# First weight tile on a second queue, an early filling matmul removed, and four output transfers halved, in a scan and gated-FFN kernel

## The chip, the cores and the metric

One core of one Trainium2 chip. The metric is the device time of one execution, in microseconds (us), from the first to the last instruction of the program. Engines are TensorE (PE), VectorE (DVE), ScalarE (ACT), GpSimd (POOL) and SyncE (SP); SP and ACT also issue transfers, which run on the core's 16 DMA engines.

## The reference

The input x is 2048 tokens of 512 values in bfloat16. It is normalised over the 512 values; from the result two branches are computed and joined:

```python
xn = _layernorm(x, axis=-1)
# s: state-space scan, 512 complex states over 2048 tokens
dt = exp(log_dt); Lam_bar = exp(dt * Lam); B_bar = ((Lam_bar - 1) / Lam)[:, None] * Bmat
Bu = einsum("bld,pd->blp", xn, B_bar)
h[t] = Lam_bar * h[t-1] + Bu[:, t]                       # for t in range(2048)
s = 2 * einsum("blp,dp->bld", h, Cmat).real + xn * Dskip
# g: gated feed-forward, inner width 1376
g = silu((gelu(xn @ w_gate) * (xn @ w_up)) @ w_down)
out = x + s * g
```

## The kernel before, in words

The 2048 tokens are cut into 4 slabs of 512 and each slab into 4 tiles of 128 (M = 4, written m; slabs are s). All weights stay in on-chip memory. A slab goes through these stages: the tiles are normalised and turned (`xna` to `xnT`, by a transposing transfer for whole slabs); gate and up products per tile (`gate_tile`, L433), multiplied on VectorE into `at`; `at` is turned to `atT` by a transposing transfer (`at_t`, L449); the down product from `atT` (L465); the state inputs (L528), rotated by tables, scanned along the tokens on VectorE (L559) and rotated back into `hst`; and the read-out (L481), multiplied by the gate and added to x (`y_part`, L486 and L491), from which a transfer writes 128 rows of the output (L494).

Nothing is scheduled while the kernel runs. Each step is recorded with what it reads and writes (`Plan.add`), and `Plan.run` emits the steps in the order of a list written out by hand, `ORDER`; the cost figures given with the steps play no part in it. So every engine has a fixed order, and an engine waits, in that order, on semaphores. Eight semaphores are shared by all transfers in the order of issue: a transfer takes the semaphore of the one eight issues before, and is issued after that one has landed.

The first slab has no time for a transposing transfer, so its head is done another way, and this is where most of the change lies:

- SP's queue starts with the loads of x tiles 0, 1 and 2, then the row tiles of `w_up` (`wu`, 128 rows of the first 1024 columns, 256 KB each; row tile k is what `up_rows(m, k)` multiplies), x tile 3, and the rest. ACT's queue starts with three small loads of the scan's parameters (`pv0`, `pv1`).
- `dummies(7, 3)` gives TensorE seven matmuls on constants from the start (L295), before any data is there.
- `center(0)` sums tile 0 in two parts, on DVE (columns 0 to c, L340) and ACT (the rest, L338), and DVE subtracts the mean (L342). `center(m)` for the other tiles sums on ACT (L346) and subtracts on DVE (L347).
- `head_t(0)` turns tile 0 by four transposes on TensorE (L312), copied out by DVE (L318) and ACT (L320) into `xcT`, a view of `W`. `parameters` turns the parameter rows (L584, L585), copied out by DVE (L587, `pf`). `fill(1, 0)` adds one matmul on constants (L301). `head_t(1)` to `head_t(3)` turn the other tiles (L327, copied by L329).
- `up_rows(m, k)` multiplies tile m by row tile k of `w_up`, two matmuls of 512 columns (L382); the sums leave by ACT (`out_up`, L391), scaled by 1/deviation, which comes later from GpSimd (`rstd`).
- After that `first_gates` does the gate products of slab 0, and its four tiles go through `at_t`.

At the end, the last tile's read-out is done in two halves of 256 columns, each with its own output transfer; `ot` has two buffers, used by even and odd tiles.

Of the kernel before, what the change touches and what calls it, by code (L numbers as in the profile page):

```python
# [10 lines left out]
AF = mybir.ActivationFunctionType  # L11
# [7 lines left out]


ORDER = (
    19, 24, 17, 18, 16, 14, 15, 13, 25, 0, 20, 12, 21, 1, 22, 2, 23, 3, 4, 27, 26, 5, 39, 6, 28, 7, 29, 41, 30, 33, 40, 60, 8, 34, 31, 61, 35, 32, 42,
    9, 63, 46, 62, 65, 133, 64, 45, 66, 131, 69, 68, 36, 37, 50, 57, 134, 51, 67, 52, 48, 10, 54, 70, 53, 49, 71, 56, 72, 73, 79, 43, 58, 76, 80, 44,
    82, 137, 77, 74, 38, 95, 147, 75, 81, 91, 78, 85, 97, 92, 55, 84, 47, 198, 135, 86, 93, 87, 59, 149, 88, 199, 151, 103, 138, 94, 83, 107, 96, 98,
    153, 216, 136, 155, 99, 101, 220, 104, 139, 11, 217, 140, 100, 109, 111, 102, 119, 106, 108, 214, 221, 105, 115, 110, 156, 132, 117, 120, 154, 90,
    218, 125, 112, 150, 116, 113, 215, 123, 114, 219, 222, 122, 141, 126, 127, 160, 164, 118, 148, 124, 89, 121, 179, 128, 143, 275, 161, 162, 165,
    158, 223, 224, 166, 163, 181, 227, 167, 129, 157, 130, 142, 152, 229, 226, 144, 183, 185, 225, 233, 168, 180, 228, 283, 280, 279, 182, 237, 159,
    169, 358, 186, 170, 184, 172, 200, 235, 171, 234, 173, 201, 241, 174, 238, 276, 243, 282, 175, 176, 258, 244, 259, 236, 277, 239, 245, 177, 278,
    178, 281, 187, 240, 246, 296, 264, 242, 202, 247, 292, 260, 284, 285, 265, 204, 188, 297, 203, 302, 262, 189, 293, 261, 191, 311, 286, 190, 248,
    303, 298, 205, 263, 192, 317, 307, 312, 300, 308, 230, 206, 299, 294, 301, 207, 295, 232, 208, 231, 305, 304, 318, 306, 352, 322, 315, 326, 209,  # L30
    210, 316, 327, 313, 320, 211, 193, 418, 309, 310, 330, 332, 212, 314, 341, 195, 331, 323, 290, 324, 328, 325, 287, 196, 337, 213, 329, 339, 288,
    197, 345, 319, 289, 353, 194, 333, 291, 146, 335, 334, 347, 354, 359, 336, 364, 338, 145, 365, 343, 360, 321, 249, 250, 355, 346, 340, 356, 342,
    376, 426, 377, 380, 366, 254, 378, 393, 381, 344, 394, 349, 382, 397, 348, 420, 350, 361, 253, 362, 351, 379, 383, 252, 398, 369, 395, 410, 421,
    251, 425, 419, 396, 256, 424, 411, 414, 435, 257, 416, 415, 357, 370, 266, 436, 443, 450, 444, 423, 417, 267, 412, 422, 375, 255, 427, 428, 269,
    445, 413, 399, 451, 429, 446, 441, 439, 460, 458, 271, 400, 440, 454, 461, 442, 270, 437, 455, 268, 448, 432, 438, 456, 481, 475, 273, 430, 465,
    452, 459, 274, 272, 471, 479, 453, 367, 371, 433, 457, 363, 480, 447, 463, 482, 462, 431, 372, 368, 434, 476, 502, 373, 484, 473, 466, 500, 503,
    384, 472, 486, 374, 492, 496, 449, 385, 493, 388, 386, 387, 501, 537, 477, 497, 474, 478, 523, 467, 483, 389, 494, 519, 498, 487, 495, 468, 524,
    499, 390, 469, 485, 525, 488, 551, 526, 489, 504, 391, 505, 520, 507, 539, 521, 552, 464, 508, 392, 522, 490, 506, 401, 513, 514, 402, 535, 403,
    553, 538, 536, 405, 406, 557, 515, 509, 555, 558, 404, 541, 569, 563, 556, 540, 408, 407, 542, 409, 554, 564, 559, 527, 565, 619, 561, 528, 562,
    560, 570, 624, 531, 530, 567, 578, 574, 575, 625, 568, 566, 576, 518, 620, 584, 577, 532, 585, 572, 510, 529, 511, 580, 591, 516, 533, 599, 582,  # L40
    583, 579, 589, 581, 571, 491, 573, 517, 587, 621, 597, 622, 586, 593, 595, 598, 600, 626, 623, 588, 629, 534, 634, 614, 615, 594, 630, 612, 543,
    596, 592, 590, 613, 544, 617, 610, 608, 604, 601, 545, 606, 635, 607, 627, 609, 605, 512, 602, 631, 603, 611, 641, 470, 616, 547, 628, 618, 639,
    548, 647, 642, 546, 643, 549, 645, 550, 636, 637, 632, 648, 646, 638, 633, 652, 640, 653, 649, 650, 657, 651, 644, 658, 654, 662, 667, 655, 656,
    663, 659, 668, 660, 664, 661, 665, 669, 666, 670, 671,
)


# [33 lines left out]
def kernel(  # L81
# [79 lines left out]
    tF = sb("tF", [P, 2, D], FP32)  # L161
    junks = [sb(f"junk{i}", [P, D]) for i in range(2)]
    junk_n = [0]

    def junk():
        junk_n[0] += 1
# [11 lines left out]
    def dve(n, emit, reads=(), writes=(), rate=1.0, base=DV, **kw):  # L178
        return pl.add(DVE, base + n / 960.0 / rate, emit, reads, writes, lag=0.13, **kw)

    def acts(n, emit, reads=(), writes=(), ptr=0, **kw):
        return pl.add(ACT, AC + 0.12 * ptr + n / 1200.0, emit, reads, writes, lag=0.16, **kw)

    def pe(n, cols, emit, reads=(), writes=(), **kw):
        return pl.add(PE, n * (cols + 6) / 2400.0, emit, reads, writes, lag=0.22, **kw)
# [4 lines left out]
    def dma(eng, issue, land, emit, reads=(), writes=(), **kw):  # L190
        return pl.add(eng, issue, emit, reads, writes, lag=land, **kw)
# [17 lines left out]
    def load_w(nm, k0, k1, c0, c1, end, landed):  # L209

        w, r = w_of[nm]
        dma_sp(end, landed, lambda: nc.sync.dma_start(out=w[:, k0:k1, c0:c1], in_=r[:, k0:k1, c0:c1]),
               [(nm, k, c) for k in range(k0, k1) for c in range(3) if c0 <= CH[c][0] < c1])
# [10 lines left out]
    load_x(0, 1.12, 2.92)  # L224
    load_x(1, 1.59, 3.35)
    load_x(2, 2.06, 3.75)
    load_w("wu", 0, 1, 0, W2, 2.53, 5.1)
    load_w("wu", 1, 2, 0, W2, 3.0, 6.3)
    load_w("wu", 2, 3, 0, W2, 3.5, 7.4)
    load_x(3, 4.0, 7.75)  # L230
# [18 lines left out]
        early.append(dve(32, lambda i=i: V.memset(at[i][:, F:FP], 0.0), writes=[("atpad", i)], rank=900.0))  # L249
    one = nc.const_aps.tensor(1.0, [P, 1], FP32)  # L250

    first = [acts(1, lambda: act(out=tiny[:], in_=one, func=AF.Silu), [], ["tiny"], rank=910.0, not_before=0.72)]
    for i, (t, v) in enumerate(((pv0[0:4, :], A_log_dt), (pv1[0:4, :], A_Lambda_im), (pv1[4:8, :], A_Lambda_re))):
        first = [dma(ACT, 0.48, 1.7, lambda t=t, v=v: A.dma_start(out=t, in_=v.rearrange("(k p) -> k p", p=P)),
                     writes=[("pv", i)], rank=900.0, not_before=0.8, after=first)]
    iota_i = sb("iota_i", [P, NBA], I32)
    iota_f = small("iota_f", NBA)

# [36 lines left out]
                T.matmul(ybank[j][:] if j < 2 else ring[i][:], lhsT=warm[:, 0:P], rhs=warm, start=True, stop=True)  # L295
        pl.add(PE, k * 0.427, f, [], [("bank", i), ("y", 0), ("y", 1)], lag=0.22, not_before=0.6)

    def fill(k, i):
        def f():
            for _ in range(k):  # L300
                T.matmul(ring[i][:], lhsT=warm[:, 0:P], rhs=warm, start=True, stop=True)  # L301
        pe(k, 512, f, [], [("bank", i)])

    def head_t(m):

        if m == 0:
# [26 lines left out]
    def center(m):  # L333

        x = x_tok[:, m, :]
        if m == 0:
            c = 3 * P
            acts(D - c, lambda: act(out=junk()[:, 0 : D - c], in_=x[:, c:D], func=AF.Copy, scale=1.0 / D, accum_out=mb[:, 0:1]),  # L338
                 [("x", 0, 0)], ["mb"], ptr=1, rank=400.0)
            dve(c, lambda: V.tensor_scalar(out=yg[0][:, 0:c], in0=x[:, 0:c], scalar1=1.0 / D, scalar2=None, op0=ALU.mult, op1=ALU.add,  # L340
                                           accum_out=ma[:, 0:1]), [("x", 0, 0)], [("yg", 0, 0), ("ma", 0)], base=0.15, rank=400.0, after=early)
            head.append(dve(512, lambda: V.tensor_scalar(out=xn[0], in0=x, scalar1=ma[:, 0:1], scalar2=mb[:, 0:1], op0=ALU.subtract, op1=ALU.subtract),  # L342
                            [("x", 0, 0), ("ma", 0), "mb"], [("xc", 0, 0), ("xc", 0, 1)], rate=2.3, rank=400.0, after=head[-1:]))
            return
        nmean, key = ma[:, m : m + 1], ("ma", m)
        sums0.append(acts(512, lambda: act(out=junk()[:], in_=x, func=AF.Copy, scale=-1.0 / D, accum_out=nmean), [("x", 0, m)], [key], ptr=2, rank=400.0 - 20 * m))  # L346
        dve(512, lambda: V.tensor_scalar(out=xn[m], in0=x, scalar1=nmean, scalar2=None, op0=ALU.add),  # L347
            [("x", 0, m), key], [("xc", m, 0), ("xc", m, 1)], rate=2.3, rank=330.0 - 20 * m)
# [123 lines left out]
    def y_part(s, m, c0, c1, bank, key, seed, e):  # L472
# [14 lines left out]
        else:  # L487
            ys = tF[:, 0, c0:c1]
            dve(w, lambda: V.tensor_tensor(out=ys, in0=ps, in1=sk[s % 2][:, m, c0:c1], op=ALU.add), [key, ("sk", s % 2, m)], [("tF",)])
            dve(w, lambda: V.tensor_tensor(out=yg[e][:, c0:c1], in0=ys, in1=g2[gi][:, b, c0:c1], op=ALU.mult), [("tF",), ("g2", gi, b)], [("yg", e, c0)])  # L490
        dve(w, lambda: V.tensor_tensor(out=ot[e][:, c0:c1], in0=yg[e][:, c0:c1], in1=x_tok[:, s * M + m, c0:c1], op=ALU.add),  # L491
            [("yg", e, c0), ("x", s, m)], [("ot", e, c0)], rate=2.0)
        mg = s * TS + m * P
        dma(SP, 0.35, 1.5, lambda: nc.sync.dma_start(out=out_td[mg : mg + P, c0:c1], in_=ot[e][:, c0:c1]), [("ot", e, c0)], [("out", s, m, c0)], svc=(2, 0.4, 0.9))  # L494

    def y_tile(s, m):
        i = y_n[0] % 2
# [143 lines left out]
    rstd(0, 1)  # L641
    for m in range(1, M):
        norms = rstd(m, m + 1)
    fill(1, 0)
    head_t(1)
    up_rows(0, 0)
    up_rows(1, 0)
# [174 lines left out]
```

## Time and profile before

| | us |
|---|---|
| median of 3 runs | 179.16 |
| lowest and highest run | 178.5, 179.44 |
| the profiled execution: its span from the first to the last instruction | 178.6 |
| time shown around that span | none |
| PE busy in it | 173.4 |
| DVE busy | 156.4 |
| ACT busy | 125.2 |
| POOL busy | 12.0 |

The profile comes from one more execution, beside the three timed ones; its span is given with one digit and has no other time beside it. Busy time of PE is that of matmuls, whose ends are modelled; instructions that issue transfers are not counted as busy. In the chain of waits each line is a stretch of the work that ended last: when it starts, how long it is, and the engine with the tile that it writes. In a timeline each line is a group of instructions with its start, its length, and in brackets the idle time of the engine before it and what ended that.

### The profile page before, as it was taken

The numbers are of one execution on the slowest core, as the hardware profiler recorded it, in microseconds if no ns is written. First come the engines' busy times: TensorE is split into PE (matmuls) and PEld (weight loads), VectorE is DVE, ScalarE is ACT, GpSimd is POOL, SyncE is SP. The second block draws the span as 40 slices with busy tenths as digits, with TensorE's granted clock in tenths as the row PEclk, the third lists the DMA queues.
The fourth block names the chain that finished last, engine by engine and source line by source line (L and its number), as shares of the span: only waits on it lengthen the run. The fifth ranks groups of instructions, "written<-read, shape, count | busy, mean of one in ns | idle before, by whom it ended". The sixth has DMA issues, their size and how long they took to land.

```text
span 178.6 us, 2428 instructions
## 1 busy us (share of the span) xinstructions
PE 173.4 (97%) x850; PEld 82.8 (46%) x850; DVE 156.4 (88%) x252; ACT 125.2 (70%) x240; POOL 12.0 (7%) x25
## 2 busy tenths in 40 slices
PE   7999999899999999999999999999999999999992
PEld 2555544344445544444445454444444455444451
DVE  3729999999599995899979999899999999999663
ACT  6679999797998999889578865373148618582340
POOL 2462040000200000000040000000000000000000
PEclk9999999999999999999999999999999999999999
DMA  5999999999000809814000075094000006536111
GB/s 159 338 372 188 176 227 315 150 211 228 2 0 0 196 2 173 110 59 81 0 0 6 6 124 129 25 195 84 0 0 0 0 29 155 69 58 135 53 64 60
DMA packets 47507, 18.66 MB, mean 104 GB/s; under 512 B 40232, under 2 KB 46472, under 8 KB 47496
## 3 DMA queue, kind: packets, MB, share of 16 engines
q1 hardware_dynamic: 47472, 18.52, 48.6%
q8 instruction: 6, 0.10, 0.3%
q14 instruction: 5, 0.04, 0.1%
q10 hardware_dynamic: 24, 0.00, 0.0%
HBM read 6.46 MB, written 2.10 MB: 48 GB/s over the span
## 4 chain that ended last, share of the span: by engine, by line
PE 81%; DVE 7%; DMA 6%; ACT 2%; POOL 0%; issue 0%; DVEq 0%
PE ring L433 31%; PE ring L465 20%; PE ybank L481 15%; PE ring L528 12%; DMA atT<-at 5%; PE ring L382 3%; ACT at L391 2%; DVE st L278 1%; DVE Q L620 1%; DMA x_tok<-in_A_x_dram 1%; DVE at L415 1%; DVE yg L486 1%; DVE tab L620 1%; DVE ot L491 1%; DVE sk L364 1%; ACT junk L351 0%
## 5 line engine op out<-in xcount | busy, mean ns | idle before, releaser
L433 PEld LDWEIGHTS <-xnT 128*128 128x128 bf16 x288 | 28.2, 98 | 28.4
L465 PE MATMUL ring<-wd,atT 128*128 128x512 bf16 (+1 forms) x176 | 39.5, 379 | 0.8 <-DMA atT<-at 0.7
L433 PE MATMUL ring<-wg,xnT 128*128 128x512 bf16 (+1 forms) x144 | 31.6, 357 | 0.0
L433 PE MATMUL ring<-wu,xnT 128*128 128x512 bf16 (+1 forms) x144 | 31.3, 357 | 0.0
L528 PE MATMUL ring<-xnT,BT 128*128 128x512 bf16 x128 | 30.1, 379 | 0.0
L559 DVE TENSOR_TENSOR_SCAN Fs<-rho,ini,W 128x512 bf16<-128x512 f32 x24 | 29.7, 1270 | 0.1
L436 ACT ACTIVATE ub<-ring 128x512 bf16<-128x512 f32 (+1 forms) x36 | 19.2, 555 | 14.1 <-PE ring L433 14.0
L481 PE MATMUL ybank<-C,hst 128*128 128x512 bf16 x120 | 27.7, 379 | 0.0
L465 PEld LDWEIGHTS <-atT 128*128 128x128 bf16 (+1 forms) x176 | 17.1, 98 | 22.1 <-DMA atT<-at 1.2
L530 ACT ACTIVATE U<-ring 128x512 bf16<-128x512 f32 x32 | 18.3, 601 | 8.0 <-PE ring L528 8.0
L436 ACT ACTIVATE gt<-ring 128x512 bf16<-128x512 f32 (+1 forms) x36 | 19.5, 555 | 3.7 <-PE ring L433 3.5
L481 PEld LDWEIGHTS <-hst 128*128 128x128 bf16 x136 | 13.3, 98 | 14.0
L528 PEld LDWEIGHTS <-BT 128*128 128x128 bf16 x128 | 12.5, 98 | 14.7
L540 DVE TENSOR_TENSOR Q<-U,tab 128x4096 bf16<-128x4096 bf16 x8 | 18.3, 2291 | 1.0 <-ACT tab L627 0.7
L468 ACT ACTIVATE g<-ring 128x512 f32<-128x512 f32 x16 | 9.3, 595 | 13.6 <-PE ring L465 13.5
L540 DVE TENSOR_TENSOR Q<-Fs,tab 128x4096 bf16<-128x4096 bf16 x8 | 18.3, 2287 | 0.1
L486 DVE TENSOR_TENSOR yg<-ybank,g 128x512 bf16<-128x512 f32 x15 | 10.2, 685 | 5.7 <-PE ybank L481 5.6
L740 ACT ACTIVATE junk<-x_tok 128x512 bf16<-128x512 bf16 x16 | 10.0, 636 | 1.2 <-DMA x_tok<-in_A_x_dram 1.2
L477 ACT ACTIVATE ybank<-sk 128x512 f32<-128x512 bf16 x15 | 9.0, 601 | 1.7 <-DVE yg L486 1.6
L745 ACT ACTIVATE xna<-x_tok,nb,rs 128x512 bf16<-128x512 bf16 x12 | 9.6, 817 | 0.0
L401 PE MATMUL ring<-wg,W 128*128 128x512 bf16 (+1 forms) x48 | 9.5, 357 | 0.0
L559 DVE TENSOR_TENSOR_SCAN Fs<-rho,W 128x512 bf16<-128x512 f32 x8 | 9.3, 1210 | 0.1
(126 smaller groups left out, 171.7 us busy)
## 6 DMA issues: line engine op xcount, KB each, us to landing
out_dram<-ot SPq DMA_DIRECT2D x15, 128.0 KB, 1.7
x_tok<-in_A_x_dram SPq DMA_DIRECT2D x3, 512.0 KB, 9.0
wg<-in_B_w_gate_dram SPq DMA_DIRECT2D x1, 1376.0 KB, 8.1
wd<-in_B_w_down_dram SPq DMA_DIRECT2D x1, 1280.0 KB, 8.7
wu<-in_B_w_up_dram SPq DMA_DIRECT2D x4, 256.0 KB, 3.6
x_tok<-in_A_x_dram SPq DMA_DIRECT2D x4, 128.0 KB, 2.3
wu<-in_B_w_up_dram SPq DMA_DIRECT2D x1, 352.0 KB
atT<-at SPq DMA_TRANSPOSE x16, 3.8
```

Of the source, the lines that this page charges most:

```text
L401: T.matmul(ps[:, 0 : b - a], lhsT=xcT[:, k, m * P : (m + 1) * P], rhs=wt[:, k, a:b], start=(k == 0), stop=(k == KT - 1))
L433: T.matmul(ps[:, 0 : b - a], lhsT=xnT[:, s % 2, m, k, :], rhs=wt[:, k, a:b], start=(k == 0), stop=(k == KT - 1))
L436: acts(b - a, lambda: act(out=dst[:, a:b], in_=ps[:, 0 : b - a], func=AF.Copy if up else AF.Gelu_apprx_tanh), [("bank", r)], [key], table= ...
L465: T.matmul(ps[:], lhsT=atT[:fs, k, m * P : (m + 1) * P], rhs=wd[:fs, k, :], start=(k == 0), stop=(k == NFT - 1))
L481: T.matmul(ps, lhsT=hst[s % 2][:, j // NPT, j % NPT, m * P : (m + 1) * P], rhs=C2[:, j // NPT, j % NPT, c0:c1], start=(j == 0 and not seed ...
L486: dve(w, lambda: V.tensor_tensor(out=yg[e][:, c0:c1], in0=ps, in1=g2[gi][:, b, c0:c1], op=ALU.mult), [key, ("g2", gi, b)], [("yg", e, c0)])
L528: T.matmul(ps[:], lhsT=BT[:, ri, k, pt * P : (pt + 1) * P], rhs=xnT[:, s % 2, :, k, :], start=(k == 0), stop=(k == KT - 1))
L530: acts(512, lambda q=q, ri=ri, ps=ps: act(out=U[ui][:, ri, q, :], in_=ps[:], func=AF.Copy), [("bank", r)], [("U", ui, q, ri)])
L540: dve(4096, lambda: V.tensor_tensor(out=Qf, in0=src.unsqueeze(1).to_broadcast(WQ), in1=table, op=ALU.mult), reads, ["Q"], rate=2.0)
L559: pl.add(DVE, 1.12 if s == 0 else 1.185, lambda ri=ri, q=q, pt=pt, first=first: V.tensor_tensor_scan(out=Fs[:, ri, q, :], data0=rho[:, pt ...
L740: acts(512, lambda i=i, fn=fn, sc=sc, m=m: act(out=junk()[:], in_=x_tok[:, s * M + m, :], func=fn, scale=sc, accum_out=sx[:, s, i, m : m + ...
L745: acts(512, lambda m=m: act(out=xn[m], in_=x_tok[:, s * M + m, :], func=AF.Identity, scale=rs[:, s, m : m + 1], bias=nb[:, s, m : m + 1]), ...
```

## The change

- The third parameter load (`A_Lambda_re`) is issued by SP instead of ACT, in the place of `w_up`'s first row tile; that row tile is issued by ACT, in the place of the parameter load.
- `fill` and its one matmul on constants are removed.
- The first sum of tile 0 is split at column 320 instead of 384 (ACT takes 192 columns instead of 128).
- `ORDER` is a new list. With the steps renumbered, the order on the engines differs in this: DVE copies the turned tile 0 (L318) ahead of the parameter copy (L587), so that after the centering of tile 1 comes tile 0's copy and then `pf`; on PE the row matmuls of tile 0 with row tile 1 come ahead of those of tile 1 with row tile 1. POOL's order is the same, and so is the rest of DVE, ACT and PE.
- Four output transfers (tiles 2 and 3 of slab 2, tiles 0 and 1 of slab 3) are each made as two halves of 256 columns, 64 KB each.
- The last two tiles write their result to the two `junk` buffers instead of the two `ot` buffers.

```diff
@@ tiles
     junks = [sb(f"junk{i}", [P, D]) for i in range(2)]
     junk_n = [0]
+    ot += junks
@@ loads on SP
     load_x(2, 2.06, 3.75)
-    load_w("wu", 0, 1, 0, W2, 2.53, 5.1)
     load_w("wu", 1, 2, 0, W2, 3.0, 6.3)
@@ loads on ACT
-    first = [acts(1, lambda: act(out=tiny[:], in_=one, func=AF.Silu), [], ["tiny"], rank=910.0, not_before=0.72)]
-    for i, (t, v) in enumerate(((pv0[0:4, :], A_log_dt), (pv1[0:4, :], A_Lambda_im), (pv1[4:8, :], A_Lambda_re))):
-        first = [dma(ACT, 0.48, 1.7, lambda t=t, v=v: A.dma_start(out=t, in_=v.rearrange("(k p) -> k p", p=P)),
-                     writes=[("pv", i)], rank=900.0, not_before=0.8, after=first)]
+    acts(1, lambda: act(out=tiny[:], in_=one, func=AF.Silu), [], ["tiny"], rank=910.0, not_before=0.72)
+    for i, (eng, nq, t, v) in enumerate(((ACT, A, pv0[0:4, :], A_log_dt), (ACT, A, pv1[0:4, :], A_Lambda_im), (SP, nc.sync, pv1[4:8, :], A_Lambda_re))):
+        dma(eng, 0.48, 1.7, lambda t=t, v=v, nq=nq: nq.dma_start(out=t, in_=v.rearrange("(k p) -> k p", p=P)), writes=[("pv", i)])
+    dma(ACT, 0.43, 3.4, lambda: A.dma_start(out=wu[:, 0, 0:W2], in_=w_of["wu"][1][:, 0, 0:W2]), writes=[("wu", 0, 0), ("wu", 0, 1)])
@@ TensorE's filling matmul
-    def fill(k, i):
-        def f():
-            for _ in range(k):
-                T.matmul(ring[i][:], lhsT=warm[:, 0:P], rhs=warm, start=True, stop=True)
-        pe(k, 512, f, [], [("bank", i)])
...
-    fill(1, 0)
     head_t(1)
@@ center(0)
-            c = 3 * P
+            c = 320
@@ y_part
-        dve(w, lambda: V.tensor_tensor(out=ot[e][:, c0:c1], in0=yg[e][:, c0:c1], in1=x_tok[:, s * M + m, c0:c1], op=ALU.add),
-            [("yg", e, c0), ("x", s, m)], [("ot", e, c0)], rate=2.0)
+        o = 2 + m % 2 if s == NS - 1 and m >= M - 2 else m % 2
+        dve(w, lambda: V.tensor_tensor(out=ot[o][:, c0:c1], in0=yg[e][:, c0:c1], in1=x_tok[:, s * M + m, c0:c1], op=ALU.add),
+            [("yg", e, c0), ("x", s, m)], [("ot", o, c0)], rate=2.0)
         mg = s * TS + m * P
-        dma(SP, 0.35, 1.5, lambda: nc.sync.dma_start(out=out_td[mg : mg + P, c0:c1], in_=ot[e][:, c0:c1]), [("ot", e, c0)], [("out", s, m, c0)], svc=(2, 0.4, 0.9))
+        cuts = (0, HD) if (NS - 2, M - 2) <= (s, m) < (NS - 1, M - 2) else (c0,)
+        for lo, hi in zip(cuts, (*cuts[1:], c1)):
+            dma(SP, 0.35, 1.5, lambda lo=lo, hi=hi: nc.sync.dma_start(out=out_td[mg : mg + P, lo:hi], in_=ot[o][:, lo:hi]), [("ot", o, c0)], [("out", s, m, lo)], svc=(2, 0.4, 0.9))
```

## The prediction

> **What bounds the kernel now.** I read the page first, then the chain that ended last in order of time, then the timeline of the first 7 us, the views by windows, and the end of SyncE's queue.
>
> From the page:
>
> ```profile
> span 178.6 us, 2428 instructions
> PE 173.4 (97%) x850; PEld 82.8 (46%) x850; DVE 156.4 (88%) x252; ACT 125.2 (70%) x240; POOL 12.0 (7%) x25
> ```
>
> TensorE is busy for 97%, so an edit can gain only before its stream starts, in its few gaps, and after its last matmul. The chain in order of time (start, length, what):
>
> ```profile
> 4.06 0.61 PE ring L312 x4
> 4.67 0.11 PE ring L584
> 4.78 0.03 PE ring L585
> 4.81 0.54 PE ring L301
> 5.35 0.43 PE ybank L327 x4
> 5.78 0.55 PE ring L382 x2
> 6.32 0.22 PE ybank L327 x4
> 6.54 4.33 PE ring L382 x20
> 10.87 0.02 issue
> 10.90 1.84 ACT at L391 x3
> ...
> 25.86 9.28 DMA atT<-at
> 35.14 0.05 issue
> 35.19 4.93 PE ring L465 x22
> ```
>
> The reader is to see three things. The filling matmul L301 stands in the chain. The same four transposes L327 take 0.43 at 5.35 and 0.22 at 6.32: TensorE runs at half pace first. From 35.19 the chain is TensorE alone until 173.44, so what the head gains or loses counts in full only if the transfer before 35.19 moves too.
>
> The timeline of the head (start, length, engine, line):
>
> ```profile
> 3.56 0.63 ACT L346 ACTIVATE junk<-x_tok 128x512 bf16<-128x512 bf16 x1 [0.26 <-DMA x_tok<-in_A_x_dram]
> 4.32 0.35 DVE L347 TENSOR_SCALAR xna<-x_tok,ma 128x512 bf16<-128x512 bf16 x1 [0.31 <-ACT junk L346]
> 4.74 0.61 PE L301 MATMUL ring<-const-bfloat16-1.0 128*128 128x512 bf16 x1
> 5.14 0.63 PE L327 MATMUL ybank<-ident,xna 128*128 128x128 bf16 x4
> ```
>
> Tile 1 was centered at 4.67 (4.32 + 0.35); its transposes began at 5.14, because the fill stood before them. But tile 1's sum (L346, 3.56) began when the second x transfer landed: x is late there, not early. And the DMA engines have no slack at that point (last columns: share of the 16 engines, GB/s):
>
> ```profile
> 2.40:2.80 0.40, 0.40 (x2) 1.00 0.98 252
> 2.80:3.20 0.40, 0.40 (x2) 1.00 0.96 273
> ```
>
> **The change, part by part.** The order of the built programs shows little more than the diff: on TensorE the fill goes and two pairs of row matmuls swap; on VectorE tile 0's copy comes ahead of the parameter copy, and the first sum is 320 columns, not 384; ScalarE's third issue is 256 KB of w_up instead of 1 KB; SyncE has 4 more output transfers. What stands in VectorE's, ScalarE's and GpSimd's streams from 7 us to 167 us is the same.
>
> *Fill.* The seven starting matmuls begin 0.427 apart (five span 2.34, one lasts 0.63: 1.71 / 4). Half pace ends where? The two row matmuls from 5.57 to the next transposes at 6.16 take 0.59, between 0.85 at half pace and 0.43 at full pace (0.216 each, by 0.863 for four later): x columns at 1.2 per ns and 1024 − x at 2.37 make 0.59 at x = 385, so the pace doubles at 5.57 + 0.32 = 5.89. If that moment stays, work taken out ahead of it is worth half: 0.43 of fill is 512 columns, 0.216 at full pace. So the gain of the fill is at most 0.2, not 0.43.
>
> *w_up row tile 0 on ScalarE's queue.* Its issue moves from 2.11 to where the third parameter load stood, 1.65: 0.46 earlier, while the second and third x transfers are under way. In 0.46 us the DMAs move 0.46 × 263 GB/s = 120 KB, so what comes behind it can be late by 0 to 0.46. The second x transfer (issued at 1.17) has a part of its packets out by then; I take 0.25, the middle, since it was issued about as long ahead of the new one as that one's whole lead. Then tile 1 is ready at 4.92, its transposes start at 4.99 and not 4.74, the row matmuls at 5.42. By 5.89 they did 564 columns, the other 460 take 0.19: they end at 6.08 instead of 6.16. Gain 0.08. With no delay: transposes 4.74, rows 5.17 to 5.96, gain 0.20. With 0.46: transposes 5.20, rows to 6.19, loss 0.03. I keep 0.08 and both ends. [...]
>
> *Parameter load on SyncE.* It moves 0.46 later (1.65 to 2.11) and queues behind three x transfers; TensorE needs it at 4.60, ahead of tile 1's transposes in its stream. The semaphore records of the trace have it landed at 3.55; 0.46 later and 0.46 more of interleaving make 4.0 to 4.5: cover 0.1 to 0.6, cost 0. If the cover goes, tile 1's transposes wait behind it. The three w_up loads, wg and the x slab behind it on SyncE keep their places: one issue goes, one comes.
>
> *Sums and copies.* 64 columns fewer save VectorE 0.07 at the first center (384 take 0.55) and add 0.05 on ScalarE, hidden by its wait to 3.56; tile 1 waits for x, so 0. The parameter copy moves behind tile 0's copy (0.28); its reader on GpSimd (5.10 to 6.13) feeds VectorE at 6.92, so 0.8 of cover, 0. Swapped row pairs: both weights are needed 0.9 later at the earliest, 0.
>
> *From the head to 35.19.* The shift passes through ScalarE (10.90, waiting for TensorE), VectorE and the transfer of 9.28. That transfer's queue is the one place where it can be lost: 0 to all; I let it pass: 0.08.
>
> *Outputs.* Four transfers of 128 KB become eight of 64 KB. An issue is 0.33 (0.43 with its wait), so 1.7 more on SyncE, hidden between 168.05 and 173.7; the last three issues (174.71, 175.37, 176.03) follow at once on VectorE as before. A half landed 1.5 after its issue; the second half of tile 2 of slab 2 would be issued at 169.25 and land at 170.8, where ot0 is written next (170.79): 0 to 0.2, with 0.5 of slack before VectorE's next wait for TensorE at 171.73. The two unshared output buffers remove waits that had ended long before: 0.
>
> *The end.* The eight DMA semaphores go round in order of issue, and at the end SyncE waits for them in pairs:
>
> ```profile
> L817 SPq EVENT_SEMAPHORE  x8: 17/28/28, 176.9 to 178.6; - x8
> SPq L817 <- DMA out_dram<-ot: 1.2, 2, 0.6
> ```
>
> The last output holds the semaphore that is second in that order: after its landing (177.57) four more waits follow, 0.062 apart (177.57 to 177.82), before the drain. With four more transfers the last output takes the last of the eight: the others have passed by then. Gain 4 × 0.062 = 0.25; ends 0.19 and 0.25, as its own wait may still be paid.
>
> *Sum:* 0.08 + 0.25 = 0.33. The profiled execution spans 178.6 (no time around it is shown, and a run of 178.5 lies below it), so it would become 178.3. It stands 0.56 under the median of the three runs, 179.16, which would become 178.8.
>
> **The rivals.**
>
> *The pace doubles later (slower).* The doubling came 5.1 after TensorE's first matmul and 1.8 after the break at 4.06. What releases it, the trace does not show. Without the fill, a late tile 1 leaves TensorE idle from 4.70 to 4.99. If a break starts the count anew, the doubling moves to 4.99 + 1.8 = 6.8, which costs (6.8 − 5.89) / 2 = 0.45; if a whole further stretch of 5.1 is needed, 2.5. It decides when the row matmuls begin no earlier than before, 5.57. For it: the fill stands just in the only free place there. Against: the break of 0.16 at 4.06 did no harm, and row matmuls take the fill's place. Time: 179.16 − 0.25 + 0.45 to 2.5 = 179.4 to 181.4, middle 180.4. [...] That the doubling is a step, and late, agrees with the rows (0.43 to 0.22).
>
> *The transfer chain moves more than the head (faster).* TensorE waits 0.69 for atT at 35.19, and that transfer takes 9.28 where the median of the 16 is 3.8. If an earlier start of the weights lets this queue drain sooner, 0.69 goes on top of the on-time head: 179.16 − 0.25 − 0.20 − 0.69 = 178.0. Against: no byte is removed.
>
> *Nothing at the head.* The x delay or that queue eats it: 178.9. *The edit does nothing at all* (the rotation of semaphores is paid elsewhere too): 179.2.
>
> **How the numbers follow.** Forecast 0.50 (178.4 to 179.0); nothing at the head 0.15; nothing at all 0.10; faster rival 0.14; slower rival 0.11. The three runs lie within 178.5 to 179.44, so about 0.5% (0.9 us) is what can be told from no change. Below 178.26: the faster rival and a little of the forecast, 0.17. Above 180.06: most of the slower one, 0.10. Within: 0.73. The range leaves out half of each extreme: from 178.0 (the faster rival) to 179.8 (the slower rival's cheaper part, from 179.4, and the upper scatter of the runs).
>
> **What would show it.** In the changed profile: L327 at 4.9 to 5.0 for tile 1, ended by VectorE's centering, ScalarE's second sum starting after 3.56, the first four-transposes group of 0.22 as early as now, TensorE's last long stretch starting at about 35.1, and one wait at most between the last landing and SyncE's drain. I am wrong if tile 1's transposes start after 5.2, if the four transposes of tile 2 still take 0.43, if the parameter transposes hold TensorE, or if the stall before 35.19 grows or vanishes.

## The result, and the profile after

The changed kernel takes 181.37 us (median of 6 runs, 180.53 to 181.55) against 179.15 us for the kernel before (6 runs, 178.50 to 179.44): ratio 1.011, 95% interval 1.0086 to 1.0133. It is 1.1% slower where a gain of 0.3 us was forecast; 181.37 lies above the range that ended at 179.8.

First a correction of the scale. Every later run gives both numbers, and the device time is the span plus about 1.8 us (the profiled execution of the changed kernel: 181.55 and 179.8). So the profile of before, with its span of 178.6, belongs to an execution of about 180.4, well above its median. A second profile of it (below) spans 177.8, with a time of 179.63. The comparisons here leave out runs over 1.5% above their kernel's fastest, and counts of runs below do the same (of the changed kernel that is one run, of 182.08).

The page of the changed kernel, its span and busy times:

```profile
span 179.8 us, 2412 instructions
PE 173.3 (96%) x833; PEld 82.8 (46%) x849; DVE 156.3 (87%) x252; ACT 125.3 (70%) x240; POOL 12.0 (7%) x25
```

Busy times are those of before, so no engine was given more to do; what changed is when TensorE works and at what pace. The timeline of its head (start, length, engine, line; line numbers are those of the changed kernel, 3 to 6 below the old ones):

```profile
1.66 0.36 ACTq L255 DMA_DIRECT2D wu<-in_B_w_up_dram  x1
2.11 0.37 SPq L254 DMA_DIRECT2D pv<-in_A_Lambda_re_dram  x1
3.34 0.63 ACT L340 ACTIVATE junk<-x_tok 128x512 bf16<-128x512 bf16 x1
...
4.24 0.17 PE L581 MATMUL ring<-ident,pv 4*128 4x4 bf16 x1
4.37 0.28 DVE L312 COPY W<-ring 128x256 bf16<-128x256 bf16 x1
5.72 0.81 SPq L213 DMA_DIRECT2D wu<-in_B_w_up_dram  x2
5.79 0.63 ACT L340 ACTIVATE junk<-x_tok 128x512 bf16<-128x512 bf16 x1 [1.73 <-DMA x_tok<-in_A_x_dram]
5.95 0.17 PE L582 MATMUL ring<-ident,pv 8*128 8x8 bf16 x1 [1.53 <-DMA pv<-in_A_Lambda_re_dram]
6.06 0.40 PE L321 MATMUL ybank<-ident,xna 128*128 128x128 bf16 x4
```

Between 4.65 and 5.72 no line starts on any engine. Tile 1 is not late: ScalarE sums it at 3.34, earlier than before (3.56), so the second x transfer was on time. Late are the third x transfer, which ScalarE waits for until 5.79, and the third parameter load, which TensorE waits for until 5.95, with tile 1's transposes (6.06; 5.14 before) queued behind it. These are two delays, and which of them counts is told by the chain below. SyncE stood still too: its next load, w_up's row tile 3, takes the semaphore of the third x transfer, and was issued at 5.72 instead of 4.01.

In the trace's transfer records the third x transfer lands at 5.71 (3.91 before), the parameter load at 5.90 (3.55), and the w_up tile, issued 0.45 earlier, at 5.52 (4.97). The windows of that stretch (the last two columns are the share of the DMA engines and GB/s):

```profile
2.80:3.20 0.40, 0.40 (x2) 0.15 (x1) 0.37 (x1) 0.38 (x2) 0.00 (x0) 1.00 0.74 126
3.20:3.60 0.40, 0.40 (x2) 0.00 (x0) 0.28 (x3) 0.34 (x2) 0.00 (x0) 1.00 0.76 182
```

Before, the same windows moved 273 and 236 GB/s. In the packet records of 2.8 to 3.6 the w_up packets on ScalarE's queue (2 KB) take 242 ns each in the first window and 137 in the second (means), and 30 packets of x (1 KB) start; before, the first window alone had 106. ScalarE's queue is not what makes those packets slow: in the kernel before the first w_up packets, on SyncE's queue, took 241 ns from 3.2 to 3.6. Why the first ones are slow is not shown.

The second loss is the pace. The windows of the changed kernel (column before the DMA share: the granted TensorE clock; it also reads 1.00 ahead of the first record, when the matmuls still go at half pace):

```profile
3.60:7.10 3.50, 1.87 (x16) 0.89 (x16) 1.53 (x6) 1.77 (x6) 0.69 (x1) 1.00 0.87 275
7.20:10.50 3.30, 3.30 (x11) 1.20 (x9) 2.87 (x11) 1.97 (x7) 1.39 (x4) 0.50 0.97 305
10.60:14.00 3.40, 3.40 (x20) 1.69 (x19) 0.35 (x1) 1.16 (x3) 2.66 (x5) 1.00 1.02 339
```

The records say: full from 3.76, half from 7.17, full from 10.58. For 3.41 us the row matmuls ran at half pace, which is worth 1.71. In the chain that ended last they are one piece, and this stands ahead of them:

```profile
1.64 4.07 DMA x_tok<-in_A_x_dram
5.79 0.73 ACT junk L340 x2
6.55 0.36 DVE xna L341
6.96 0.45 PE ybank L321 x4
7.42 6.41 PE ring L376 x22
```

So the chain runs through the third x transfer: tile 2 is summed at 5.79, centered at 6.55 and turned at 6.96. It does not run through the parameter load, although TensorE's one long wait is for it: what stands behind that wait, tile 1's transposes and the first row matmuls, was done at 6.88 (6.29 + 0.59), 0.08 before tile 2's transposes started. The two delays end at nearly the same time. The chains of the two later profiles of this kernel also run through the third x transfer; the one of the loads-only version below runs through the parameter load.

The first gate products start at 18.00, against 15.46 in the first profile of before and 15.79 in the second. Against the second, the +2.21 is the same at TensorE's last matmul (176.55, 174.34). The first profile's wait for `atT`, 0.7 up to 35.19, is not in the second. It comes in some executions: a third profile of the changed kernel has 0.5 of it, and most other profiles have none.

The end did as forecast. From the end of TensorE's last matmul to the end of the span it is 3.46 and 3.48 in the two profiles of before and 3.21 in the changed kernel:

```profile
L813 SPq EVENT_SEMAPHORE  x8: 17/28/28, 177.8 to 179.7; - x8
```

The last output landed at 178.94, 0.78 ahead of the end of SyncE's last wait at 179.72 (before: 177.56 and 1.02).

### The profile page after: what moved, and what is told of

It reads as the page before. It is cut to its first block, busy times and chain, and to the rows that moved or that the text cites. A ratio compares the mean times of both kernels' runs of the same rounds, so it can differ in the third digit from the quotient of the medians.

```text
span 179.8 us, 2412 instructions
## 1 busy us (share of the span) xinstructions
PE 173.3 (96%) x833; PEld 82.8 (46%) x849; DVE 156.3 (87%) x252; ACT 125.3 (70%) x240; POOL 12.0 (7%) x25
## 4 chain that ended last, share of the span: by engine, by line
PE 93%; DMA 2%; DVE 2%; issue 1%; SPq 0%; ACT 0%; DVEq 0%; ACTq 0%
PE ring L427 31%; PE ring L459 21%; PE ring L525 15%; PE ybank L475 14%; PE ring L395 6%; PE ring L376 4%; DMA x_tok<-in_A_x_dram 2%; PE ybank L376 1%; DVE yg L480 1%; DVE junk L486 1%; SPq L222 0%; ACT junk L340 0%; PE ybank L321 0%; DVE xna L341 0%; DVEq L480 0%
## 5 line engine op out<-in xcount | busy, mean ns | idle before, releaser
L459 PE MATMUL ring<-wd,atT 128*128 128x512 bf16 (+1 forms) x170 | 38.9, 379 | 0.3
```

Source lines behind the costliest of these rows:

```text
L459: T.matmul(ps[:], lhsT=atT[:fs, k, m * P : (m + 1) * P], rhs=wd[:fs, k, :], start=(k == 0), stop=(k == NFT - 1))
```

## The experiments

Theories at the start. A: the exchange of the two loads is the cause. B: the missing filling matmul lets TensorE fall idle, and the clock comes late. C: both, the delay of the loads and a clock that this idle stretch costs. All kernels were timed beside the kernel before, whose medians in the four sittings were 179.15, 179.36, 179.45 and 179.19; ratios are to those.

**The parts alone.** The kernel before with only the two loads exchanged, the filling matmul kept:

```diff
-                lambda: nc.sync.dma_start(out=w[:, k0:k1, c0:c1], ...)
+                lambda: (A if (nm, k0, k1) == ("wu", 0, 1) else nc.sync).dma_start(out=w[:, k0:k1, c0:c1], ...)
-    A.dma_start(out=t, in_=v.rearrange(...))
+    (nc.sync if i == 2 else A).dma_start(out=t, in_=v.rearrange(...))
```

> Kernel before with only the two loads exchanged: first w_up row tile issued third on ScalarE, third parameter load in its place on SyncE; fill, sums, order and outputs as before. Theory A (the exchange is the cause: in the changed kernel the parameter load landed at 5.90 and the third x transfer at 5.71, and TensorE waited 1.5 for the former): most of the loss appears here, 180.8 to 182, tile 1's transposes at about 6, a wait of about 1.2 to 1.5 on the parameter load after the parameter transposes. Rival B (the missing fill is the cause, by the clock): within 0.4 of the kernel before, since the fill is still there. Rival C (neither alone, only together): between, 179.5 to 180.5, the fill taking up a part of the wait.

Measured: 182.0, ratio 1.0113 (1.0063 to 1.0162), as much as the whole change. Its timeline on TensorE:

```profile
6.05 0.18 PE L585 MATMUL ring<-ident,pv 8*128 8x8 bf16 x1 [1.36 <-DMA pv<-in_A_Lambda_re_dram]
6.17 0.61 PE L301 MATMUL ring<-const-bfloat16-1.0 128*128 128x512 bf16 x1
6.57 0.63 PE L327 MATMUL ybank<-ident,xna 128*128 128x128 bf16 x4
```

The filling matmul stands behind the parameter transposes and so cannot fill the wait; the clock's first record of full speed is at 9.47.

The kernel before without the filling matmul:

```diff
-    fill(1, 0)
+    fill(0, 0)
```

> Kernel before with only the filling matmul left out. Theory A: the fill costs at most what the prediction said, so 178.9 to 179.2, tile 1's transposes at 4.75. Rival B (the fill keeps the pace up): 180 to 181.5, with a second stretch of slow matmuls or a later doubling.

Measured: 179.14, ratio 0.9997 (0.998 to 1.0013), tile 1's transposes at 4.44. B falls: no idle stretch opens, since the row matmuls move up into the place.

The kernel before with the output part alone (halved transfers, two more buffers):

```diff
+    ot += junks
...
+        o = 2 + m % 2 if s == NS - 1 and m >= M - 2 else m % 2
+        cuts = (0, HD) if (NS - 2, M - 2) <= (s, m) < (NS - 1, M - 2) else (c0,)
...
```

> Kernel before with only the output part of the change: four halved outputs and the two extra output buffers. By the prediction's term: 0.25 faster, 178.9, last landing to the end 0.78 instead of 1.05. Rival (halves cost SyncE or the transfers time): 179.2 or more.

Measured: 179.07, ratio 1.0005 (0.9983 to 1.0027). The end after the last matmul is 3.22, but a quarter of a microsecond does not show in the times.

The changed kernel with both loads put back (`ORDER` is changed to match):

```diff
-    ... (SP, nc.sync, pv1[4:8, :], A_Lambda_re) ...
+    ... (ACT, A, pv1[4:8, :], A_Lambda_re) ...
-    dma(ACT, 0.43, 3.4, lambda: A.dma_start(out=wu[:, 0, 0:W2], ...
+    dma(SP, 0.43, 3.4, lambda: nc.sync.dma_start(out=wu[:, 0, 0:W2], ...
```

> Changed kernel with only the two loads put back to their queues of before. Theory A: all of the loss goes and the small gains stay, 178.5 to 179.0. Rival B: it stays above 180.5. Rival C: 179.2 to 180.5.

Measured: 179.02, ratio 0.9981 (0.996 to 1.0002). The whole loss is in the loads.

**Which load, and by which path.** The parameter load back on ScalarE ahead of the w_up tile, which is then ScalarE's fourth (issued at 2.92):

```diff
-    19, 20, 21, 23, 24, 0, ...  2, 41, 22, 3, 4,
+    19, 20, 21, 22, 23, 24, 0, ...  2, 41, 3, 4,
-    ... (SP, nc.sync, pv1[4:8, :], A_Lambda_re) ...
+    ... (ACT, A, pv1[4:8, :], A_Lambda_re) ...
```

> Changed kernel with the third parameter load back on ScalarE, ahead of the w_up tile there; SyncE issues no parameter load. Theory A1 (the late parameter load stops TensorE, which takes its instructions in order): the wait of 1.5 at the parameter transposes goes and tile 1's transposes start at about 4.5 to 4.7; but the third x transfer still lands at 5.5 or later, so tile 2 is late as before: 180 to 180.8, half of the loss. Rival A2 (the parameter load is all of it): 178.5 to 179.2. Rival A3 (the late x and w_up transfers alone set it): no change from the changed kernel, 181.4.

Measured: 182.69, ratio 1.0193 (1.015 to 1.0236), later than all three theories had it. Parameters and tile 1 are on time, the third x transfer lands at 4.61, and TensorE now waits for the w_up tile itself (what is waited for, us, times, longest), which lands at 7.74, behind the two row tiles on SyncE's queue (5.47 and 7.54):

```profile
PE ring L376 <- DMA wu<-in_B_w_up_dram: 2.5, 1, 2.5
```

The same with the parameter load left on SyncE, the w_up tile issued behind tile 0's sum (2.96):

```diff
-    19, 20, 21, 23, 24, 0, 26,
+    19, 20, 21, 24, 0, 26, 23,
```

> Changed kernel with the w_up tile issued on ScalarE behind tile 0's sum (about 2.9 instead of 1.66), so that the three x transfers and the parameter load have their packets out first. Theory A (interleaving with the x transfers): third x transfer lands at 3.9 to 4.1, the parameter load at 4.1 to 4.4, tile 1's transposes at 4.5 to 4.7, first row matmuls at about 5.5 when the w_up tile lands: 178.8 to 179.4. Rival (a second queue is slow by itself, whatever it meets): x and the parameter load as late as in the changed kernel or the w_up tile after 6.5: 181 or more.

Measured: 181.82, ratio 1.0122 (1.0072 to 1.0172): the third x transfer lands at 3.96, the parameters at 4.14, both in time, and the w_up tile at 7.01, for a wait of 2.0. So the tile on ScalarE's queue hurt at each place: early, x and the parameters came late (5.71 and 5.90), later it came itself behind SyncE's weights (7.01 and 7.74).

The parameter load alone on SyncE, w_up's first row tile on SyncE behind it:

```diff
-    19, 20, 21, 23, 24, 0, ...  2, 41, 22, 3, 4,
+    19, 20, 21, 24, 0, ...  2, 41, 22, 23, 3, 4,
-    dma(ACT, 0.43, 3.4, lambda: A.dma_start(out=wu[:, 0, 0:W2], ...
+    dma(SP, 0.43, 3.4, lambda: nc.sync.dma_start(out=wu[:, 0, 0:W2], ...
```

> The changed kernel, but w_up's first row tile is issued by SyncE again, right behind the third parameter load; ScalarE issues two loads only. Theory A (what makes tile 2's x and the parameter load late is the 256 KB of weights on a queue of their own): the third x transfer lands at 3.9 to 4.1, the parameter load at 4.1 to 4.6, tile 1's transposes start by 4.8, the weight tile lands 0.4 later than in the kernel before (about 5.4) and the first row matmuls wait for it: 179.0 to 179.8. Rival (the parameter load's place on SyncE's queue, behind three x transfers, is enough): it lands after 5.3, tile 1's transposes after 5.4, the clock is late or taken back as in the changed kernel: 180.5 or more.

Measured: 178.81, ratio 0.9978 (0.9944 to 1.0013). Ten of its runs lie at 178.5 to 179.2 and two at 181.0. The third x transfer lands at 3.95 and the parameters at 4.02, in time: the parameter load's place is harmless.

```profile
4.81 0.41 PE L321 MATMUL ybank<-ident,xna 128*128 128x128 bf16 x4
5.85 0.59 PE L376 MATMUL ring<-wu,W 128*128 128x512 bf16 x2 [0.63 <-DMA wu<-in_B_w_up_dram]
```

Half of the w_up tile (128 KB) on ScalarE's queue, the other half on SyncE behind the parameter load:

```diff
-    A.dma_start(out=wu[:, 0, 0:W2], in_=w_of["wu"][1][:, 0, 0:W2])
+    A.dma_start(out=wu[:, 0, 0:TS], in_=w_of["wu"][1][:, 0, 0:TS])
...
+            if (nm, k0, k1) == ("wu", 1, 2):
+                nc.sync.dma_start(out=w[:, 0, TS:W2], in_=r[:, 0, TS:W2])
```

> The changed kernel, but ScalarE issues only the first 512 columns of w_up's first row tile (128 KB); the other 512 are issued by SyncE behind the third parameter load. Theory A (interleaving by bytes): half the bytes beside tile 2's x transfer delay it by half as much: it lands at 4.6 to 4.9 in place of 5.71 (3.91 before), the parameter load at 4.8 to 5.1, TensorE's wait at the parameter transposes is 0.5 to 0.8 in place of 1.53, and the time is 179.6 to 180.6. Rival (any transfer on the second queue at that moment holds back a whole round, whatever its size): third x transfer after 5.4, wait above 1.2, time 181 or more.

Measured: 179.44, ratio 1.0015 (0.9983 to 1.0046). The third x transfer lands at 4.62 and TensorE waits 0.34 for the parameters, less than either theory said. Eight runs lie at 179.1 to 179.5, four at 180.6 to 181.0. With nothing, 128 KB and 256 KB issued on ScalarE's queue 0.02 behind it, that transfer landed at 3.86 to 4.02 (4.61 in the version where the tile came at 2.92), at 4.62, and at 4.96 to 5.81. In all nine profiles with a tile there it landed 0.18 to 0.23 after that tile: issued ahead of the other transfer, it came behind the whole of it.

**The path through TensorE's order.** The changed kernel with the parameter transposes and their copy moved behind tile 1's first row matmuls, and to another bank (not in the lines shown):

```diff
-    ... 27, 28, 29, 30, 33, 32, 46, 45, 40, 60, 31, 62, 34, 42, 64, 61, 63, 67,
+    ... 27, 28, 29, 30, 32, 46, 45, 40, 60, 31, 62, 42, 64, 61, 63, 33, 34, 67,
```

> Changed kernel with the parameter transposes and their copy moved behind the first row matmuls of tile 1 on TensorE (and to another bank); all loads as in the changed kernel. A1: tile 1's transposes at 4.4 to 4.6, then TensorE waits for w_up's first tile (5.5) and for tile 2's x (5.7): 180 to 180.8. A2: 178.5 to 179.2. A3: 181.4.

Measured: 180.44, ratio 1.0077 (1.005 to 1.0104), no clear gain. In its profile tile 1's transposes start at 4.49 and nothing waits for the parameters. So the parameters are not the only way in, as the changed kernel's own chain says. The next in TensorE's order is tile 2, whose x was at 4.96 in this execution, with a wait of 0.27, and would leave TensorE idle for 1 or more where it lands as late as 5.7; that is argued, and no profile of this version shows it.

**The clock.** Filling matmuls between the two parameter transposes of the changed kernel, where TensorE waits; all else is unchanged, the late loads too:

```diff
+            for _ in range(4):
+                T.matmul(ring[0][:], lhsT=warm[:, 0:P], rhs=warm, start=True, stop=True)
             T.transpose(pt_ps[:, 4:12], pv1[:, :], ident[0:8, 0:8])
```

> Changed kernel with four filling matmuls between the two parameter transposes, where TensorE waits about 1.5. Theory C (a part of the loss is the clock: in the changed kernel's profile it was granted at 3.76, taken back from 7.17 to 10.58): the granted clock is not taken back, and the median falls by 0.3 to 1.2, to 180.2 to 181. Rival (the clock has no share in the median): 181.4, or later by what the four matmuls overhang.

Measured: 179.91, ratio 1.0028 (1.0004 to 1.0052). Its transposes still wait, to 5.38, and the third x transfer lands at 5.12, but the clock, full from 4.04, stays full. Much of the loss is the clock's: the ratio's interval lies clear of the first timing's (1.0086 to 1.0133), though it overlaps that of the later timing below (1.0033 to 1.0105).

The changed kernel and the kernel before, each profiled once more:

> The changed kernel once more, for a second profile. Theory (the idle 1.5 at the parameter transposes costs the clock): tile 1's transposes start after 5.2 again, and the record of the granted clock has a half-speed stretch of 3.41 behind a first full one, or the full clock starts later than 6.5. Rival (the stretch taken back was chance in the one profile): full clock from 6.0 or earlier, without a break, and the same time of 180.5 to 181.6.

> The kernel before once more, for a second profile. Theory (the moment of the full clock is not tied to the kernel's own start but falls where a running window of 3.41 ends): the full clock starts elsewhere than at 5.88, anywhere from 3.5 to 7, and the span moves with it by half of the difference, from 177.4 (clock at 3.5) to 179.1 (clock at 6.9). Rival (it comes 5.1 after TensorE's first matmul): full clock at 5.8 to 6.0 again, whatever the span.

The changed kernel came at 179.53, with TensorE's wait again (timeline):

```profile
5.54 0.17 PE L582 MATMUL ring<-ident,pv 8*128 8x8 bf16 x1 [1.05 <-DMA pv<-in_A_Lambda_re_dram]
5.65 0.40 PE L321 MATMUL ybank<-ident,xna 128*128 128x128 bf16 x4
5.88 0.59 PE L376 MATMUL ring<-wu,W 128*128 128x512 bf16 x2
6.54 0.40 PE L321 MATMUL ybank<-ident,xna 128*128 128x128 bf16 x4
6.88 4.92 PE L376 MATMUL ring<-wu,W 128*128 128x512 bf16 x22
```

The 22 row matmuls take 4.92 (4.86 in the chain, where they took 6.41): the clock is full from 4.08, nothing is taken back, and the time is lower by 2. Neither expectation holds as a whole: the theory had the clock taken back, the rival had the time unchanged. The kernel before came at 179.63 with full clock from 5.57, 0.31 earlier than in its first profile: outside the rival's 5.8 to 6.0, but by little. Its span is 0.8 shorter, not the 0.15 that half of 0.31 would give, so most of that difference is not the clock's. Over all profiles with the same seven starting matmuls the first full clock came anywhere from 3.57 to 6.47 (and once at 9.47), with the same code ahead of it. So the changed kernel's loss could be a mixture. More runs of it, and fewer filling matmuls in the wait:

> The changed kernel itself, for the spread of its times. Theory C2 (a mixture: the direct delay of about 0.5, and in most executions a stretch of 3.41 at half pace, worth 1.7): two groups, a smaller one at 179.3 to 179.9 and a larger one at 180.5 to 181.8, with few runs between. Rival (a steady delay of the loads): one group about 181.2, within 0.6 to each side.

> The changed kernel with one filling matmul between the two parameter transposes, so that the idle stretch there is 0.2 to 0.4 shorter (1.2 to 1.3 in place of 1.5). Theory C2: the same two groups as in the changed kernel, the slow one smaller than there but at the same times; median 179.8 to 181.2. Rival (a steady delay): no change against the changed kernel, 181.2 within 0.3, one group.

> The changed kernel with two filling matmuls between the two parameter transposes: idle 0.7 to 1.0. Theory C2: the slow group has at most a third of the runs, median 179.4 to 180.2, as with four (179.91). Rival (a steady delay): 181.2 within 0.3, and four filling matmuls would have helped for another reason.

| filling matmuls in the wait | median | ratio (95%) | runs at 180.5 or more |
|---|---|---|---|
| none (first timing) | 181.37 | 1.011 (1.0086 to 1.0133) | 6 of 6 |
| none (again) | 180.76 | 1.0069 (1.0033 to 1.0105) | 5 of 9 |
| none (second profile) | 179.53 | | 0 of 1 |
| one | 180.12 | 1.0053 (1.0026 to 1.0081) | 4 of 12 |
| two | 179.84 | 1.0046 (1.002 to 1.0072) | 2 of 12 |
| four | 179.91 | 1.0028 (1.0004 to 1.0052) | 2 of 12 |

For the changed kernel the 11 runs at 180.5 or more have a median of 181.25, the 5 below it 179.53: 1.72 apart, half of 3.41. That speaks for the mixture, though these two groups are not cleanly parted (180.23, 180.53 and two of 180.76 lie between); those of the half tile and of the parameter load alone, above, are, by 1.1 and 1.8. Of the kernel before, 3 of 107 runs in the four sittings were that late. The share of late runs falls from 11 of 16 to 4 and 2 of 12 with the filling matmuls, which a steady delay would not do; within the one sitting it is 5 of 9, 4 of 12 and 2 of 12, too few to be told apart by themselves.

For each run the mean granted clock is on record too, in which a stretch of 3.41 at half pace shows as 0.990 or 0.991 (1.71 of 180). Of the 11 late runs two show it, those of 181.55 and 181.12. The other nine have 1.0. A run whose first full clock only comes late can have 1.0 too, since time ahead of the first record reads as 1.00: the profiled run of the loads-only version, with its first full clock at 9.47 and a time of 182.09, does. In those nine, then, nothing of that length was taken back; that the first full clock came late in them is inferred from their times, and no profile of the changed kernel shows it.

Whether the clock, once granted, was lost again can be set beside TensorE's busy time in the 3.41 us behind the first full clock. The windows of the changed kernel, where it was taken back, and of its second profile, where it was kept:

```profile
3.76:7.17 3.41, 1.78 (x17) 0.95 (x16) 1.44 (x6) 1.68 (x6) 0.76 (x1) 1.00 0.86 268
```

```profile
4.08:7.49 3.41, 2.29 (x19) 1.18 (x18) 1.92 (x8) 2.12 (x7) 1.03 (x1) 1.00 0.90 286
```

It was taken back also at 0.99 and 1.39 (the two versions with the w_up tile issued later) and kept at 2.48, 2.73, 2.78, 2.95 and 3.35. So in these nine profiles it was taken back at 1.78 busy of 3.41 and less and kept at 2.29 and more; what decides it, they do not show. Nor do they show what decides when full clock first comes. Measured are these (matmuls run from 0.76 on): the loads-only version, busy for 1.99 of the 3.41 up to 6.05, had none until 9.47; the version with the parameter transposes moved, busy for 2.30 of the 3.41 up to 3.06, had none until 6.47; the version without the filling matmul had it at 3.57, after 2.81 of 3.41, and the second profile of the kernel before at 5.57, after 3.40.

**A better version?** The parameter load alone on SyncE, with one filling matmul ahead of the first row matmuls:

```diff
+            if (m, k) == (0, 0):
+                T.matmul(ps[0][:], lhsT=warm[:, 0:P], rhs=warm, start=True, stop=True)
```

> The version with the parameter load alone moved to SyncE (w_up's first row tile on SyncE behind it), and one filling matmul ahead of the first row matmuls, where TensorE waited 0.63 for that tile. Theory C2: no run at 180.5 or above (2 of 12 without the filling matmul), fast runs as without it, 178.5 to 179.2, median 178.6 to 179.0. Rival (the two runs at 181.0 had another cause than TensorE's idle time): one or two runs of 12 above 180.5 again.

Measured: 179.22, ratio 0.9985 (0.9958 to 1.0011); none of the 11 runs counted at 180.5 or more, but a twelfth, outside the count, was 181.3; that the late group is emptied is not shown. This version, its sibling without the filling matmul (178.81) and the changed kernel with the loads put back (179.02) all beat the changed kernel, and none can be told from the kernel before.

## Why the prediction was wrong

- **The w_up tile on ScalarE's queue: the step that failed.** "In 0.46 us the DMAs move 0.46 × 263 GB/s = 120 KB, so what comes behind it can be late by 0 to 0.46." Only the bytes of the lead were counted, where the tile shared the engines for as long as it lasted (45 of its packets and 30 of x began from 2.8 to 3.6): 256 KB, while the rate fell to 126 and 182 GB/s. And the allowance went to the wrong transfer. I took the second x transfer 0.25 late; it was on time (3.32). The one at risk was the third, issued 0.02 ahead of the tile: 1.8 late in the first profile, 1.4 in the two others, and in all three the chain runs through it. Even the late end of the estimate, a loss of 0.03, was far too little: the loads alone cost 1.1% (1.0113).
- **The parameter load on SyncE: the same step again.** "0.46 later and 0.46 more of interleaving make 4.0 to 4.5: cover 0.1 to 0.6, cost 0." The first 0.46 was right: with the w_up tile off ScalarE's queue the load lands at 4.02, 0.47 later than before, and its place costs nothing (0.9978). With the tile there it landed at 5.90, so the interleaving was 1.88 and not 0.46. The sentence "if the cover goes, tile 1's transposes wait behind it" is what happened; it was given no price. By the chain the wait itself added almost nothing to the third x transfer's delay: tile 2 came 0.08 later still, and the version with the parameter transposes moved behind is not clearly faster.
- **"Keep their places" on SyncE.** SyncE's later loads kept their order and not their time: row tile 3 was issued 1.7 later, through the shared semaphore. No wait for it shows on TensorE.
- **The rival of the later pace: right mechanism, wrong trigger, wrong weight.** Its price (0.45 to 2.5) holds the 1.71 found, but I tied it to the missing filling matmul, which alone does nothing. The trigger is TensorE's idle stretch of 1.5, at a wait that another term had called free. At 0.11 it had too little chance.
- **"If that moment stays."** The doubling was read as one moment, 5.89, and each early microsecond ahead of it priced at a half. That moment moves by 2.9 us over the profiles, from 3.57 to 6.47 (and once 9.47), so it keeps no fixed distance from the kernel's start. Nor was it final: in the first profile of the changed kernel, with a wait of 1.53 in the 3.41 behind that moment, the clock was taken back for 3.41; in the second, with a wait of 1.05, it was not.
- **The base.** "No time around it is shown" led me to set a span beside a median of times that are 1.78 longer; the profile was a late execution, and the wait before 35.19 that fed the faster rival is in some executions only.
- **Right:** the filling matmul (0.2 at most; the ratio without it is 0.9997), sums, copies and outputs at nothing that the runs can show, and the end, where 0.25 was forecast and 3.46 became 3.21.

## What to carry to other kernels

A load that is moved to a second queue need not land earlier: the w_up tile, issued 0.45 earlier into engines that in the kernel before were busy at 0.98 and 0.96 from 2.40 to 3.20, landed 0.55 later (5.52, 4.97). Count its whole size against every transfer that is in flight (the third x transfer, 3.91 to 5.71), and then against the small one behind those (the parameter load, 3.55 to 5.90), since an engine with a fixed order stops at whichever lands last, as TensorE did here for 1.53. Ask what the main engine does in the longest wait that an edit can open: here a delay worth a few tenths (179.53, the median of the runs that were not late, against 179.2) became two microseconds (181.55) where TensorE lost the clock behind that wait, or, as the times of most late runs suggest, got it late. And a stall that one profile shows, like the 0.7 up to 35.19 in the first profile of before, may be missing in the next: take a second profile before a gain is worked out from it.

## What the runs showed of the hardware

- Full clock came at another time in each profile: in three profiles of the changed kernel it was first full at 3.76, 4.08 and 4.54. Only in the first, busy for 1.78 of the next 3.41 us (2.29 and 2.48 in the others), was it taken back, and it came again after 3.41 more (3.76, 7.17, 10.58).
- Two profiles of the kernel before had full clock from 5.88 and from 5.57, which is worth 0.15, and their spans differ by 0.8: the moment of full clock alone does not explain how much this kernel's times spread.
- The end of the program depended on which of the eight shared semaphores the last output took, and so on how many transfers there were in all. SyncE waited for them in a fixed order, about 0.06 each. After the last output's landing four more of these waits follow in the kernel before, which ends 3.45 to 3.48 after the last matmul in the four profiles with 60 transfers (two of it, two of versions of it); three follow in the half-tile version with 65 (3.38); none follows in the thirteen profiles with 64 (3.20 to 3.23).
